# Retention in 128-token chunks with carried states, x^T kept in SBUF, and attention interleaved with the expert matmuls

## The chip, the cores and the metric

The kernel runs on one core of a Trainium2 chip. The metric is the device time of one execution in microseconds (us), taken as the median of several runs. The profile is one execution; its span, from the first to the last instruction, is the scale of all times below that carry a position ("at 62 us"). PE is TensorE's matmul stream and PEld its weight loads, DVE is VectorE, ACT is ScalarE, POOL is GpSimd, and SP is SyncE, which here only issues transfers. A letter q (SPq, POOLq) means the sequencer of that engine.

## The reference, cut to what matters

Retention with a decay per head gives x, and x goes through four experts, weighted by normalised probabilities.

```python
# q, k, v: (8 batches, 8 heads, 576 tokens, 64), float32
scores = (1 / sqrt(64)) * q @ k^T
Dmat   = where(i >= j, gamma[h] ** (i - j), 0)         # causal decay
x      = ((scores * Dmat) @ v) -> (4608 tokens, 512)   # heads side by side
p      = probs / (probs.sum(-1) + 1e-9)                # (4608, 4)
out    = sum over e of p[:, e] * (relu(x @ w1[e]) @ w2[e])   # w1 512x1024, w2 1024x512
```

There is no softmax. The decay factors into a part that belongs to the query and a part that belongs to the key, so retention is linear: the tokens before a chunk act on it only through a 64x64 state per head, the sum of k^T v. The changed kernel rests on this.

## The kernel before

The kernel has two stages with DRAM between them. The first computes the whole lower triangle of scores head by head, with 128x128 blocks, and writes x to DRAM. The second reads x back transposed, 512 tokens at a time, and runs the experts.

```python
x_dram = dram.tile([N_moe, Dm], BF16)
for e in range(E):                       # all eight expert matrices first, on POOL
    nc.gpsimd.dma_start(out=wt1, in_=moe_w1[e]...); nc.gpsimd.dma_start(out=wt2, in_=moe_w2[e]...)
for h in range(H):
    # [cut] load q, k (SP) and v (POOL) of this head for all batches; scale by decay; transpose
    for b in range(B):
        for jb in range(n_sblk):         # 5 key blocks
            while off < Ni:              # all queries after the block
                ps = psum_sc.tile([128, 512], FP32, tag="psc")
                nc.tensor.matmul(ps[:tj, :nn], lhsT=kT[:, j0:j0 + tj], rhs=qT[...])
                rr_copy(s_sbuf[:tj, off:off + nn], ps[:tj, :nn])     # ACT and DVE in turn
            nc.vector.tensor_mul(s_sbuf[:tj, :tj], s_sbuf[:tj, :tj], ltri[:tj, :tj])
        for ib in range(n_sblk):
            for jb in range(ib + 1):
                nc.tensor.matmul(out_p[:ti, :D], lhsT=s_sbufs[jb][...], rhs=vv(jb, 0, tj))
            rr_copy(out_sb[:ti, ib * D:(ib + 1) * D], out_p[:ti, :D])
        nc.sync.dma_start(out=x_dram[...], in_=out_sb[...])
for nt in range(n_ntiles):               # 9 blocks of 512 tokens
    for dc in range(n_dchunk):
        nc.sync.dma_start_transpose(out=t[:, :nn], in_=x_dram[n0:n0 + nn, ...])
    # [cut] experts: 8 groups of 4 matmuls (ph), relu on ACT, 4 groups of 8 matmuls (po),
    #       acc += p * po on DVE (ACT for expert 0), store
```

Of the kernel before, what the change touches and what calls it, by code (L numbers as in the profile page):

```python
# [9 lines left out]
FP32 = mybir.dt.float32  # L11
F32R = mybir.dt.float32r
BF16 = mybir.dt.bfloat16
FP8 = mybir.dt.float8e4
Copy = mybir.ActivationFunctionType.Copy
Relu = mybir.ActivationFunctionType.Relu
Exp = mybir.ActivationFunctionType.Exp


@with_exitstack  # L20
def kernel(
# [10 lines left out]
    nc = tc.nc  # L32

    B, H, S, D = q.shape
    N_moe, E = moe_domain_probs.shape
    E_, Dm, F = moe_w1.shape
    assert E == E_
    assert Dm == H * D
    assert N_moe == B * S

    scale = 1.0 / math.sqrt(D)

    dram = ctx.enter_context(tc.tile_pool(name="dram", bufs=1, space=bass.MemoryType.DRAM))
    x_dram = dram.tile([N_moe, Dm], BF16)

    SBLK = 128
    n_sblk = (S + SBLK - 1) // SBLK
    sblk_sizes = [min(SBLK, S - i * SBLK) for i in range(n_sblk)]
    sblk_starts = [i * SBLK for i in range(n_sblk)]

    DCHUNK = 128
    n_dchunk = Dm // DCHUNK
    FCHUNK = 128
    n_fchunk = F // FCHUNK

    wpool = ctx.enter_context(tc.tile_pool(name="wpool", bufs=1))

    actx = ExitStack()
    const = actx.enter_context(tc.tile_pool(name="const", bufs=1))
    ident = const.tile([128, 128], BF16)  # L60
    make_identity(nc, ident)
    ltri = const.tile([128, 128], BF16)
    nc.gpsimd.memset(ltri, 1.0)
    nc.gpsimd.affine_select(out=ltri, in_=ltri, compare_op=mybir.AluOpType.is_ge, fill=0.0,
                            base=0, channel_multiplier=-1, pattern=[[1, 128]])

    gamma_pool = actx.enter_context(tc.tile_pool(name="gamma", bufs=1))
    qk_pool = actx.enter_context(tc.tile_pool(name="qk", bufs=2))
    psum_tr = actx.enter_context(tc.tile_pool(name="psum_tr", bufs=2, space=bass.MemoryType.PSUM))
    psum_sc = actx.enter_context(tc.tile_pool(name="psum_sc", bufs=3, space=bass.MemoryType.PSUM))  # L70
    psum_out = actx.enter_context(tc.tile_pool(name="psum_out", bufs=3, space=bass.MemoryType.PSUM))
    sbuf_bh = actx.enter_context(tc.tile_pool(name="sbuf_bh", bufs=2))
    sc_pool = actx.enter_context(tc.tile_pool(name="sc_pool", bufs=2))

    iota_tile = gamma_pool.tile([128, 1], FP32, tag="iota")
    nc.gpsimd.iota(iota_tile, pattern=[[0, 1]], base=0, channel_multiplier=1,
                   allow_small_or_imprecise_dtypes=True)
    gq_cache = {}
    gk_cache = {}
    for h in range(H):  # L80
        gamma = 1.0 - 2.0 ** (-5.0 - h)
        lg = math.log(gamma)
        for sb in range(n_sblk):
            s0 = sblk_starts[sb]
            bq = gamma_pool.tile([128, 1], FP32, tag=f"bq_{h}_{sb}")
            nc.vector.memset(bq, lg * s0 + math.log(scale))
            gq = gamma_pool.tile([128, 1], FP32, tag=f"gq_{h}_{sb}")
            nc.scalar.activation(gq, iota_tile, Exp, scale=lg, bias=bq)
            bk = gamma_pool.tile([128, 1], FP32, tag=f"bk_{h}_{sb}")
            nc.vector.memset(bk, -lg * s0)  # L90
            gk = gamma_pool.tile([128, 1], FP32, tag=f"gk_{h}_{sb}")
            nc.scalar.activation(gk, iota_tile, Exp, scale=-lg, bias=bk)
            gq_cache[(h, sb)] = gq
            gk_cache[(h, sb)] = gk

    w1_sb = {}
    w2_sb = {}
    for e in range(E):
        wt1 = wpool.tile([128, n_dchunk, F], BF16, tag=f"w1_{e}", name="wt1")
        nc.gpsimd.dma_start(out=wt1, in_=moe_w1[e].rearrange("(dc p) f -> p dc f", p=128))  # L100
        w1_sb[e] = wt1
        wt2 = wpool.tile([128, n_fchunk, Dm], BF16, tag=f"w2_{e}", name="wt2")
        nc.gpsimd.dma_start(out=wt2, in_=moe_w2[e].rearrange("(fc p) d -> p fc d", p=128))
        w2_sb[e] = wt2

    NB2 = B // 2
    _ci = [0]

    def rr_copy(out_, in_):
        i = _ci[0] % 2  # L110
        _ci[0] += 1
        if i == 0:
            nc.scalar.activation(out_, in_, Copy)  # L113
        else:
            nc.vector.tensor_copy(out_, in_)  # L115

    for h in range(H):
        qT_big = [sbuf_bh.tile([128, S], BF16, tag=f"qT{bb}", name=f"qT{bb}") for bb in range(NB2)]
        kT_big = [sbuf_bh.tile([128, S], BF16, tag=f"kT{bb}", name=f"kT{bb}") for bb in range(NB2)]
        v_raw = {}  # L120
        for sb in range(n_sblk):
            s0 = sblk_starts[sb]
            ts = sblk_sizes[sb]

            def load_scaledT(src, gtile, name, dst):
                raw = qk_pool.tile([128, B, D], FP32, tag=f"{name}_raw{sb}")
                nc.sync.dma_start(out=raw[:ts], in_=src[:, h, s0:s0 + ts, :].rearrange("b s d -> s b d"))
                scaled = qk_pool.tile([128, B * D], BF16, tag=f"{name}_s{sb}")
                nc.scalar.activation(scaled[:ts], raw[:ts].rearrange("p b d -> p (b d)"), Copy,  # L129
                                     scale=gtile[:ts, :])  # L130
                for bb in range(NB2):
                    pt = psum_tr.tile([128, 128], BF16, tag="pt")
                    nc.tensor.transpose(pt[:128, :ts], scaled[:ts, bb * 128:(bb + 1) * 128], ident[:ts, :ts])  # L133
                    rr_copy(dst[bb][:128, s0:s0 + ts], pt[:128, :ts])

            load_scaledT(q, gq_cache[(h, sb)], "q", qT_big)
            load_scaledT(k, gk_cache[(h, sb)], "k", kT_big)

            vr = qk_pool.tile([128, B, D], BF16, tag=f"v_raw{sb}")
            nc.gpsimd.dma_start(out=vr[:ts], in_=v[:, h, s0:s0 + ts, :].rearrange("b s d -> s b d"))  # L140
            v_raw[sb] = vr.rearrange("s b d -> s (b d)")

        for b in range(B):
            bb = b // 2
            ph = (b % 2) * 64
            qT = qT_big[bb][ph:ph + 64, :]
            kT = kT_big[bb][ph:ph + 64, :]

            def vv(sb, r0, rn):
                return v_raw[sb][r0:r0 + rn, b * D:(b + 1) * D]  # L150

            out_sb = sbuf_bh.tile([128, n_sblk * D], BF16, tag="out_sb")
            s_sbufs = []
            for jb in range(n_sblk):
                j0 = sblk_starts[jb]
                tj = sblk_sizes[jb]
                Ni = S - j0
                s_sbuf = sc_pool.tile([128, S], BF16, tag=f"ssb{jb}")
                off = 0
                while off < Ni:  # L160
                    nn = min(512, Ni - off)
                    ps = psum_sc.tile([128, 512], FP32, tag="psc")
                    nc.tensor.matmul(ps[:tj, :nn], lhsT=kT[:, j0:j0 + tj],  # L163
                                     rhs=qT[:, j0 + off:j0 + off + nn], start=True, stop=True)
                    rr_copy(s_sbuf[:tj, off:off + nn], ps[:tj, :nn])
                    off += nn
                nc.vector.tensor_mul(s_sbuf[:tj, :tj], s_sbuf[:tj, :tj], ltri[:tj, :tj])  # L167
                s_sbufs.append(s_sbuf)
            for ib in range(n_sblk):
                i0 = sblk_starts[ib]  # L170
                ti = sblk_sizes[ib]
                out_p = psum_out.tile([128, D], FP32, tag="po")
                for jb in range(ib + 1):
                    j0 = sblk_starts[jb]
                    tj = sblk_sizes[jb]
                    i_off = i0 - j0
                    nc.tensor.matmul(out_p[:ti, :D], lhsT=s_sbufs[jb][:tj, i_off:i_off + ti],  # L177
                                     rhs=vv(jb, 0, tj),
                                     start=(jb == 0), stop=(jb == ib))
                rr_copy(out_sb[:ti, ib * D:(ib + 1) * D], out_p[:ti, :D])  # L180
            n_full = S // SBLK
            rem = S - n_full * SBLK
            nc.sync.dma_start(
                out=x_dram[b * S:b * S + n_full * SBLK, h * D:(h + 1) * D].rearrange("(sb p) d -> p sb d", p=SBLK),
                in_=out_sb[:SBLK, :n_full * D].rearrange("p (sb d) -> p sb d", d=D))
            if rem > 0:
                nc.sync.dma_start(
                    out=x_dram[b * S + n_full * SBLK:b * S + S, h * D:(h + 1) * D],
                    in_=out_sb[:rem, n_full * D:n_full * D + D])

    actx.close()

    NTILE = 512
    n_ntiles = (N_moe + NTILE - 1) // NTILE
# [98 lines left out]
```

## Time and profile before

| what | before |
|---|---|
| time, median (range) | 893.84 us (893.67 to 896.29) |
| span, granted clock | 893.0 us, 1.000 |
| start, PE mostly idle | 0 to 76 us |
| attention | 76 to 384 us |
| round trip of x | 384 to 391 us |
| experts | 391 to 889 us |

The first fence is the windows view of the kernel before. Each line is a stretch of time, its length, then busy time and count of instructions of PE, PEld, DVE, ACT and POOL, then granted clock (the share of TensorE's full clock that it was given), the mean busy share of the DMA engines (which can exceed 1 where transfers overlap), and GB/s.

```profile
0.00:30.00 30.00, 1.97 (x9) 0.97 (x10) 3.23 (x84) 19.24 (x88) 10.51 (x20) 1.00 1.08 185
30.00:60.00 30.00, 3.24 (x13) 1.36 (x13) 1.44 (x7) 5.42 (x14) 4.83 (x6) 1.00 1.27 192
60.00:76.00 16.00, 7.42 (x39) 3.30 (x39) 4.25 (x21) 6.46 (x21) 0.93 (x2) 1.00 1.56 169
76.00:384.00 308.00, 265.30 (x1604) 130.66 (x1603) 170.65 (x803) 171.91 (x553) 25.18 (x30) 1.00 0.52 75
384.00:391.00 7.00, 3.72 (x8) 1.10 (x9) 0.00 (x0) 0.00 (x0) 0.00 (x0) 1.00 0.40 86
391.00:889.00 498.00, 497.75 (x2297) 225.00 (x2295) 96.94 (x215) 196.49 (x324) 0.00 (x0) 1.00 0.09 27
```

Three stages have three limits. Until 76 us the DMA is full and PE waits. From 76 to 384 us PE is busy 86% of the time, with 1604 small matmuls. From 391 us PE is never idle, and DVE and ACT are busy only 19% and 39% of that time, so there is room for other work beside the experts.

The second fence is the chain of waits of the kernel before where the stages meet: start, length, what, and how many instructions.

```profile
388.75 2.63 DMA t<-x_dram
391.42 7.23 PE ph L240 x24
398.65 6.91 PE po L249 x32
```

Thirty-two matmuls of 512 columns take 6.91 us, that is 216 ns each. There are 2304 of them, hence 497 us, which the change does not touch. Everything else in the kernel, 396 us of 893, is what a change can win.

### The profile page before, as it was taken

How to read it: one execution, taken by the hardware profiler on the slowest of the kernel's cores; microseconds unless marked ns; L12 is line 12 of the kernel's file. 1: busy time of each engine (PE TensorE's matmuls, PEld its weight loads, DVE VectorE, ACT ScalarE, POOL GpSimd, SP SyncE). 2: the span in 40 equal slices, each digit the busy share in tenths (PEclk: the TensorE clock that was granted, in tenths of full speed). 3: DMA queues.
4: the chain of work that ended last, by engine and by line, in shares of the span. 5: the costliest groups of instructions: out<-in, count | busy, mean ns of one | idle time of the engine just before them, and what ended most of it. 6: DMA issues, size and time to landing. Idle time of an engine off the chain costs nothing.

```text
span 893.0 us, 11224 instructions
## 1 busy us (share of the span) xinstructions
PE 779.4 (87%) x3968; PEld 362.4 (41%) x3968; DVE 277.3 (31%) x1128; ACT 399.5 (45%) x997; POOL 41.5 (5%) x57
## 2 busy tenths in 40 slices
PE   0016998988788898989999999999999999999998
PEld 0003444444344444434444444444444444444443
DVE  1004555656455554532202212022130211302112
ACT  8125766664646444434352442534425334243342
POOL 4110101011010100000000000000000000000000
PEclk9999999999999999999999999999999999999999
DMA  9999479393945510120110201002020020200101
GB/s 181 199 175 178 75 108 123 73 120 80 114 81 54 44 17 11 21 55 2 36 36 0 72 1 49 23 1 71 1 60 13 1 70 1 71 1 1 47 1 48
DMA packets 187704, 51.67 MB, mean 58 GB/s; under 512 B 176896, under 2 KB 180992, under 8 KB 187648
## 3 DMA queue, kind: packets, MB, share of 16 engines
q1 hardware_dynamic: 143872, 37.84, 20.5%
q0 software_dynamic: 43776, 13.11, 13.5%
q8 instruction: 31, 0.51, 0.2%
q14 instruction: 25, 0.20, 0.1%
HBM read 45.16 MB, written 14.16 MB: 66 GB/s over the span
## 4 chain that ended last, share of the span: by engine, by line
PE 74%; issue 10%; DMA 9%; ACT 4%; DVE 1%; POOL 1%; SPq 1%; POOLq 0%; ACTq 0%
PE ph L240 28%; PE po L249 28%; PE ps L163 9%; PE out_p L177 6%; DMA vr<-in_v_dram 5%; PE pt L133 3%; DMA wt_419<-in_moe_w_dram 2%; ACT s_sbuf L113 2%; DMA raw<-in_k_dram 1%; POOL vr L140 0%; SPq L212 0%; DMA t<-x_dram 0%; DVE s_sbuf L115 0%; DVE s_sbuf L167 0%; DVE out_sb L115 0%
## 5 line engine op out<-in xcount | busy, mean ns | idle before, releaser
L244 ACT ACTIVATE hT<-ph 128x512 bf16<-128x512 f32 x288 | 171.8, 597 | 264.4 <-PE ph L240 264.4
L257 DVE SCALAR_TENSOR_TENSOR acc<-po,p_t,acc 128x512 f32<-128x512 f32 x108 | 81.0, 750 | 378.8 <-PE po L249 378.8
L249 PEld LDWEIGHTS <-hT 128*128 128x128 bf16 x1152 | 112.8, 98 | 135.8
L133 PE MATMUL pt<-ident,scaled 128*128 128x128 bf16 (+1 forms) x320 | 69.5, 269 | 87.9 <-ACT scaled L129 17.9
L177 PE MATMUL out_p<-vr,s_sbuf 128*128 128x64 bf16 (+2 forms) x960 | 113.2, 242 | 6.0 <-ACT out_sb L113 5.0
L177 PEld LDWEIGHTS <-s_sbuf 128*128 128x128 bf16 (+2 forms) x960 | 70.2, 127 | 86.9 <-issue 49.3
L113 ACT ACTIVATE s_sbuf<-ps 128x512 bf16<-128x512 f32 (+2 forms) x192 | 74.7, 391 | 67.5 <-PE ps L163 63.6
L115 DVE CAST s_sbuf<-ps 128x64 bf16<-128x64 f32 (+2 forms) x192 | 80.5, 427 | 13.1 <-PE ps L163 8.7
L133 PEld LDWEIGHTS <-scaled 128*128 128x128 bf16 (+1 forms) x320 | 32.0, 115 | 109.0 <-issue 85.4
L240 PE MATMUL ph<-t,wt_415 128*128 128x512 bf16 x288 | 67.7, 393 | 3.9 <-DMA t<-x_dram 3.9
L240 PE MATMUL ph<-t,wt_427 128*128 128x512 bf16 x288 | 63.6, 379 | 0.0
L249 PE MATMUL po<-wt_417,hT 128*128 128x512 bf16 x288 | 63.6, 379 | 0.0
L249 PE MATMUL po<-wt_421,hT 128*128 128x512 bf16 x288 | 63.6, 379 | 0.0
L240 PE MATMUL ph<-t,wt_419 128*128 128x512 bf16 x288 | 63.6, 379 | 0.0
L249 PE MATMUL po<-wt_425,hT 128*128 128x512 bf16 x288 | 63.6, 379 | 0.0
L240 PE MATMUL ph<-t,wt_423 128*128 128x512 bf16 x288 | 63.6, 379 | 0.0
L249 PE MATMUL po<-wt_429,hT 128*128 128x512 bf16 x288 | 63.6, 379 | 0.0
L167 DVE TENSOR_TENSOR s_sbuf<-s_sbuf,ltri 128x128 bf16<-128x128 bf16 (+1 forms) x320 | 59.3, 208 | 11.8 <-ACT s_sbuf L113 9.9
L115 DVE CAST out_sb<-out_p 128x64 bf16<-128x64 f32 (+1 forms) x160 | 34.1, 218 | 66.1 <-PE out_p L177 60.3
L113 ACT ACTIVATE out_sb<-out_p 128x64 bf16<-128x64 f32 (+1 forms) x160 | 34.3, 222 | 35.3 <-PE out_p L177 26.1
L140 POOL DMA_DIRECT2D vr<-in_v_dram x40 | 33.6, 854 | 265.7 <-PE pt L133 117.0
L240 PEld LDWEIGHTS <-wt_415 128*128 128x128 bf16 x288 | 28.9, 101 | 41.1 <-issue 9.4
(159 smaller groups left out, 471.8 us busy)
## 6 DMA issues: line engine op xcount, KB each, us to landing
out_dram<-acc SPq DMA_DIRECT2D x36, 256.0 KB, 2.1
raw<-in_q_dram SPq DMA_DIRECT2D x32, 256.0 KB, 5.3
raw<-in_k_dram SPq DMA_DIRECT2D x32, 256.0 KB, 5.6
vr<-in_v_dram POOLq DMA_DIRECT2D x32, 128.0 KB, 6.8
x_dram<-out_sb SPq DMA_DIRECT2D x64, 64.0 KB, 1.8
wt_415<-in_moe_w_dram POOLq DMA_DIRECT2D x1, 1024.0 KB, 10.7
wt_417<-in_moe_w_dram POOLq DMA_DIRECT2D x1, 1024.0 KB, 16.5
wt_419<-in_moe_w_dram POOLq DMA_DIRECT2D x1, 1024.0 KB, 21.4
```

Source lines behind the costliest of these rows:

```text
L113: nc.scalar.activation(out_, in_, Copy)
L115: nc.vector.tensor_copy(out_, in_)
L133: nc.tensor.transpose(pt[:128, :ts], scaled[:ts, bb * 128:(bb + 1) * 128], ident[:ts, :ts])
L140: nc.gpsimd.dma_start(out=vr[:ts], in_=v[:, h, s0:s0 + ts, :].rearrange("b s d -> s b d"))
L163: nc.tensor.matmul(ps[:tj, :nn], lhsT=kT[:, j0:j0 + tj], rhs=qT[:, j0 + off:j0 + off + nn], start=True, stop=True)
L167: nc.vector.tensor_mul(s_sbuf[:tj, :tj], s_sbuf[:tj, :tj], ltri[:tj, :tj])
L177: nc.tensor.matmul(out_p[:ti, :D], lhsT=s_sbufs[jb][:tj, i_off:i_off + ti], rhs=vv(jb, 0, tj), start=(jb == 0), stop=(jb == ib))
L240: nc.tensor.matmul(ph[:128, :nn], lhsT=w1e[:, dc, fc * FCHUNK:(fc + 1) * FCHUNK], rhs=xt_tiles[dc][:, :nn], start=(dc == 0), stop=(dc == n ...
L244: nc.scalar.activation(hT[:, fc, :nn], ph[:, :nn], Relu)
L249: nc.tensor.matmul(po[:nsn, :], lhsT=hT[:, fc, ns * NSUB:ns * NSUB + nsn], rhs=w2e[:, fc, :], start=(fc == 0), stop=(fc == n_fchunk - 1))
L257: nc.vector.scalar_tensor_tensor(acc_tiles[ns][:nsn, :], po[:nsn, :], p_tiles[ns][:nsn, e:e + 1], acc_tiles[ns][:nsn, :], op0=mybir.AluOpT ...
```

## The change

The intent is to do less attention work, to drop the DRAM copy of x, and to put attention into the gaps of DVE and ACT beside the experts. Retention is done in chunks of 128 tokens: scores only inside a chunk, and a state carried from chunk to chunk. Two heads share one PE array: score matmuls use one half of its rows each (64x128), output matmuls one half of its columns each (128x64). Outputs come out transposed, so they go straight into x^T. Attention of batch nt+1 is cut into 19 units, one placed after every second expert group of block nt.

```diff
-    x_dram = dram.tile([N_moe, Dm], BF16)
+    xT = const.tile([128, NDC, N], BF16)
...
+        def U_kv(n, pairs):          # state: k^T v of chunk n added up in PSUM, copied by ACT
+            nc.tensor.matmul(kvp[g][:, p, :], lhsT=km[:, n, ...], rhs=vm[:, n, ...], ...)
+            nc.scalar.activation(sbd[n][j:j + 64, a:z, j:j + 64], kvp[g][...], Copy)   # j = 0, 64
+        def U_T(p):                  # 8 transposes of q and k for a pair of heads
+            nc.tensor.transpose(pt[:, i, c * C:(c + 1) * C], src[:, c, ...], ident)
+            nc.vector.tensor_copy(qkT[:, :, p, 0:SM], pt)
+        def U_S(p):                  # scores inside the chunks
+            for c in range(NC_):
+                for j in range(2):   # two heads, two row halves of the array
+                    r = slice(64 * j, 64 * j + 64)
+                    nc.tensor.matmul(s[j][:, c, :], lhsT=qkT[r, 1, p, cs], rhs=qkT[r, 0, p, cs])
+            nc.vector.tensor_tensor(st[:, j], s[j], tri..., op=MULT)
+        def U_O(p):                  # scores x v, plus state x q; decay on the way out
+            nc.tensor.matmul(o[64 * j:64 * j + 64, ...], lhsT=vm[:, c, 2 * p + j, :], rhs=sT[p][:, j, c, :])
+            nc.tensor.matmul(o[:, ...], lhsT=sbd[c - 1][:, p, :], rhs=qkT[:, 0, p, ...])
+            nc.vector.tensor_tensor(xT[:, p, b * S:b * S + SM], o, gq[:, p, 0:SM], op=MULT)
...
-            nc.sync.dma_start_transpose(out=t[:, :nn], in_=x_dram[n0:n0 + nn, ...])
+    att = attention(0)               # batch 0 alone, before the experts
+    for nt in range(n_nt):
+        nxt = attention(nt + 1) if nt + 1 < B else None
+        if nxt is not None and nt + 2 < B:
+            load(nt + 2)
+        for _ in moe(nt):            # yields after each of 48 expert groups
+            n += 1
+            if nxt is not None and n >= 3 and n % 2 == 1:
+                next(nxt, None)
```

The four further matmul groups for the last 64 tokens of a batch (576 = 4 x 128 + 64) are cut here. Loads also change: q, k and v now come batch by batch. Batch 0 comes by SP in 128 KB pieces and is cast by ACT, DVE and POOL; later batches' k comes by SP, their q and v by POOL. The eight expert matrices are still issued by POOL at the very start. PSUM now gives three buffers instead of eight to the experts.

## The prediction

> **What bounds the kernel now.** By the windows view there are three stages. (1) To about 76 us, the DMA: PE is busy 22 of the first 90 us. Eight weight loads (16.8 MB of f32 source) are issued in 9 us and land 5.7 to 6.7 us apart until 57 us; the 256 KB q/k loads, in 256-byte rows, then land every 7 to 9 us, and every 2.7 us afterwards, beside v. (2) 76 to 384 us: attention, PE 86% busy with small matmuls, an eviction and a mask after each. (3) 391 to 889 us: the experts. The chain of waits shows blocks of 32 matmuls at 6.91 us without a gap (216 ns each; 2304 of them, 497 us). The change leaves this work as it is.
>
> **What it removes.** Stage 2 as a stage (308 us) and the round trip of x (385 to 391 us). The chunked form has about 152 small matmuls per batch, against 1664 in all (3968 - 2304 on the page). They run between expert groups, where DVE (18% busy in stage 3) and ACT (40%) have room.
>
> **What it costs on PE.** Five back-to-back 128x64 matmuls take 0.45 us against 0.24 for one (52 ns each); two transposes 0.37 to 0.40 against 0.27 (100 to 130 ns). My estimate is 80 ns: 152 x 0.08 = 12.2 us per batch, plus 1.3 for changes of array shape. The Trainium skill, "TensorEngine Tiling (Array Packing)", Key Properties, says that changing the tiling mode drains the engine; no duration of it can be read here. So 13.5 us per batch; batches 1 to 7 are on the PE path: 94 us.
>
> **The start**, the weak part. Batch 0 needs 3.1 MB on the SP queue in competition with the same weights. The Trainium skill, "DMA: Bandwidth & Descriptors", Issuing engines are not separate DMA queues, says that all queues interleave on the same 16 engines; this trace agrees (7 to 9 us per load beside the weights, 2.7 after). By 58 us some 9 of its 12 x 256 KB are there, the rest by 65 us. In the built order a DVE multiply of batch 1's k stands before batch 0's last x^T write, and PE has batch 1's state matmuls (needing its v) before the first expert group's end. So the experts wait for batch 1's k and v too: the probabilities come as 4608 pieces of 16 bytes ahead of k, and Pool issues v only after its casts. Some 17000 pieces at 195 GB/s of 256 bytes (both queues after 57 us) are 22 us: the experts start in earnest at about 88 us.
>
> **Sum.** 88 start + 494 experts (some are done earlier) + 94 attention + 8 PE bubbles (three PSUM buffers, not eight) + 4 tail = 688 us. Range 655 to 730. Chances: faster by over 2% 0.98, within 2% 0.01, slower 0.01.
>
> **What would show each step.** Windows: PE continuously busy only from 80 to 100 us. Waits: DVE's k multiply of batch 1 waits for its DMA, PE behind it. A block of 512 tokens takes 66 to 73 us, the last one 55 to 56; 512-column matmuls keep 216 ns. DMA nearly idle after 130 us.
>
> **What would make it wrong.** Attention matmuls cheaper by overlapping array tiles (8 us per batch: 650) or dearer by drains (18 us: 720); expert groups waiting for evictions behind attention work on DVE; later q/v loads, issued by Pool one head at a time (0.9 us each), coming too late; a start at 70 or 110 us.

## The result

The changed kernel takes 641.61 us (median of 4 runs, 640.12 to 642.94); the kernel before took 893.75 us (893.47 to 896.29) in the same rounds. The ratio is 0.7175, with a 95% interval from 0.7158 to 0.7192, and the output is correct. Here and below a ratio is the mean time of one kernel's fast runs over that of the kernel before's fast runs of the same rounds, so it is not quite the ratio of the medians. The direction was predicted, but 641.6 lies below the predicted range of 655 to 730 and 46 us below the predicted sum of 688.

The span is 638.6 us. PE's busy line on the page, first before and then after, shows that PE fell by 212 us and now fills 89% of a shorter span.

```profile
PE 779.4 (87%) x3968; PEld 362.4 (41%) x3968; DVE 277.3 (31%) x1128; ACT 399.5 (45%) x997; POOL 41.5 (5%) x57
```

```profile
PE 567.1 (89%) x3454; PEld 270.7 (42%) x3520; DVE 205.3 (32%) x345; ACT 228.2 (36%) x422; POOL 105.3 (16%) x150
```

(66 of 3520 matmul records are missing after; their weight loads are all there.)

The next fence is the windows view after, with the same columns as before.

```profile
50.00:60.00 10.00, 0.00 (x0) 0.00 (x0) 0.29 (x2) 0.63 (x1) 0.61 (x1) 1.00 1.23 211
60.00:70.00 10.00, 6.03 (x40) 3.07 (x41) 4.93 (x13) 4.00 (x17) 9.09 (x13) 1.00 1.54 146
70.00:80.00 10.00, 6.79 (x80) 4.06 (x80) 7.23 (x13) 3.48 (x16) 6.99 (x10) 1.00 1.82 174
80.00:90.00 10.00, 9.77 (x61) 4.95 (x62) 3.02 (x6) 5.59 (x11) 8.25 (x12) 0.83 1.85 176
150.00:250.00 100.00, 99.19 (x643) 47.89 (x654) 38.40 (x60) 40.46 (x74) 19.93 (x27) 1.00 0.43 52
```

PE is busy without a break from 80 us on. Between 150 and 250 us, in the middle of attention and experts together, it is 99% busy; so beside the experts no eviction holds it up.

How long is a block of 512 tokens? The first expert's results leave PSUM through an ACT instruction that writes acc, and its first occurrence marks each block. The timeline of ACT shows it for two early blocks and for the last two.

```profile
153.04 0.69 ACT L352 ACTIVATE acc<-po,probs 128x512 f32<-128x512 f32 x1 [0.94 <-PE po L348]
216.45 0.69 ACT L352 ACTIVATE acc<-po,probs 128x512 f32<-128x512 f32 x1 [0.94 <-PE po L348]
...
532.81 0.69 ACT L352 ACTIVATE acc<-po,probs 128x512 f32<-128x512 f32 x1 [1.13 <-PE po L348]
588.07 0.69 ACT L352 ACTIVATE acc<-po,probs 128x512 f32<-128x512 f32 x1 [1.13 <-PE po L348]
```

A block with attention in it takes 63.41 us (153.04 to 216.45), and one without takes 55.26 (532.81 to 588.07), which is 256 matmuls of 216 ns. So attention costs 8.16 us per batch, bubbles included. With seven such batches, 57.1 us; nine bare blocks, 497.3 us; the last matmul's end at 634.65; this leaves 80.3 us as the effective start, by which I mean everything on PE's path that is neither an expert block nor attention of batches 1 to 7.

Where the 8.16 us go is read from the chain of waits after, inside one block. These lines are samples of all groups; the lines between them are cut.

```profile
227.24 0.45 PE pt L220 x8
227.69 1.73 PE ph L341 x8
229.41 0.16 PE s_1951 L242
229.57 0.05 PE s_1951 L242
229.63 0.05 PE s_1951 L242
229.69 0.05 PE s_1951 L242
232.44 0.34 PE o L267 x8
232.78 0.27 PE o L271 x3
238.69 0.86 PE ph L341 x4
239.55 0.22 PE kvp L207 x4
241.83 1.83 PE ph L341 x8
```

Eight transposes take 0.45 us and four state matmuls 0.22, that is 56 ns each. Eight score matmuls, of which the chain shows one of each pair, take about 0.33. Eight output matmuls take 0.34 and the three state outputs after them 0.27. Eight 512-column matmuls take 1.73 us after transposes but 1.83 after scores (the score group before 241.83 is cut): the way back from the half-array shape costs 0.1 us. The timeline of PE shows the pairs of score matmuls, on the two row halves, starting together, within 10 ns:

```profile
229.41 0.22 PE L242 MATMUL s_1951<-qkT 64*128 64x128 bf16 x1
229.41 0.22 PE L242 MATMUL s_1952<-qkT 64*128 64x128 bf16 x1
229.47 0.22 PE L242 MATMUL s_1951<-qkT 64*128 64x128 bf16 x1
229.47 0.22 PE L242 MATMUL s_1952<-qkT 64*128 64x128 bf16 x1
```

The start is read from the waits of the changed kernel (in total, how often, longest) and from ACT's timeline.

```profile
ACT qm L192 <- DMA raw_q<-in_q_dram: 39.0, 3, 21.1
PE kvp L207 <- ACT sbd_158 L213: 24.1, 1, 24.1
PE kvp L207 <- DMA vm<-in_v_dram: 2.3, 2, 1.3
```

```profile
58.53 0.63 ACT L192 ACTIVATE qm<-raw_q 128x512 bf16<-128x512 f32 x1 [21.12 <-DMA raw_q<-in_q_dram]
62.18 0.63 ACT L192 ACTIVATE qm<-raw_q 128x512 bf16<-128x512 f32 x1 [3.02 <-DMA raw_q<-in_q_dram]
62.71 0.43 ACT L213 ACTIVATE sbd_158<-kvp 64x64 bf16<-64x64 f32 x2
```

In the built order ACT has all four casts of batch 0's q ahead of the first copy of a state (sbd). The last q lands at 62.2 us, so PE stands from 39 to 63 us and then needs about 17 us for batch 0's attention. The last of the three waits is for batch 1's v: until 80.0 us, state matmuls of batch 1 stand on PE between those of batch 0, and PE waits 2.3 us for their v.

### The profile page after: what moved, and what is told of

Its sections match the earlier page's. It is cut to its first block, busy times and chain, and to the rows that moved or that the text cites. A ratio compares the mean times of both kernels' runs of the same rounds, so it can differ in the third digit from the quotient of the medians.

```text
span 638.6 us, 8366 instructions
## 1 busy us (share of the span) xinstructions
PE 567.1 (89%) x3454; PEld 270.7 (42%) x3520; DVE 205.3 (32%) x345; ACT 228.2 (36%) x422; POOL 105.3 (16%) x150
## 4 chain that ended last, share of the span: by engine, by line
PE 86%; SPq 8%; DMA 3%; issue 1%; POOL 1%; DVE 0%; ACT 0%; ACTq 0%; POOLq 0%
PE po L348 39%; PE ph L341 39%; SPq L79 8%; PE pt L220 2%; PE o L267 2%; DMA vm<-in_v_dram 1%; PE o L271 1%; PE kvp L207 1%; DMA qm<-in_q_dram 1%; DMA raw_v<-in_v_dram 1%; POOL qm L101 1%; PE ptr L229 0%; DVE sTr L259 0%; PE orem L280 0%; PE orem L284 0%
## 5 line engine op out<-in xcount | busy, mean ns | idle before, releaser
L354 DVE SCALAR_TENSOR_TENSOR acc<-po,probs,acc 128x512 f32<-128x512 f32 x108 | 81.1, 751 | 197.8 <-PE po L348 177.6
L341 PE MATMUL ph<-xT,wt_166 128*128 128x512 bf16 x277 | 67.7, 385 | 1.3 <-issue 0.6
L341 PE MATMUL ph<-xT,wt_178 128*128 128x512 bf16 x281 | 68.0, 380 | 0.4
L341 PE MATMUL ph<-xT,wt_174 128*128 128x512 bf16 x277 | 67.5, 380 | 0.5
L101 POOL DMA_DIRECT2D qm<-in_q_dram x56 | 41.6, 775 | 158.4 <-PE pt L220 156.2
L341 PE MATMUL ph<-xT,wt_182 128*128 128x512 bf16 x279 | 66.7, 380 | 0.5
L348 PE MATMUL po<-wt_184,hT 128*128 128x512 bf16 x283 | 63.4, 379 | 0.3
L101 POOL DMA_DIRECT2D vm<-in_v_dram x56 | 41.7, 771 | 60.5 <-PE o L271 58.2
L223 DVE COPY qkT<-pt 128x1024 bf16<-128x1024 bf16 x32 | 22.0, 688 | 90.8 <-PE pt L220 90.8
L220 PE MATMUL pt<-ident,qm 128*128 128x128 bf16 x128 | 13.4, 229 | 34.0 <-ACT qm L192 34.0
L341 PEld LDWEIGHTS <-wt_166 128*128 128x128 bf16 x288 | 27.7, 99 | 31.0 <-issue 1.8
L207 PE MATMUL kvp<-vm,km 128*128 128x128 bf16 x128 | 15.5, 225 | 27.4 <-ACT sbd_158 L213 24.1
L341 PEld LDWEIGHTS <-wt_182 128*128 128x128 bf16 x288 | 26.8, 98 | 29.3
L341 PEld LDWEIGHTS <-wt_174 128*128 128x128 bf16 x288 | 26.4, 98 | 28.8
L341 PEld LDWEIGHTS <-wt_178 128*128 128x128 bf16 x288 | 26.4, 98 | 28.5
L352 ACT ACTIVATE acc<-po,probs 128x512 f32<-128x512 f32 x36 | 24.7, 687 | 36.9 <-PE po L348 36.9
L185 DVE TENSOR_TENSOR km<-raw_k,gk 128x512 bf16<-128x512 f32 (+1 forms) x44 | 22.0, 557 | 36.8 <-DMA raw_k<-in_k_dram 19.6
```

What stands on the lines that cost most here:

```text
L101: nc.gpsimd.dma_start(out=m[:, :, h, :], in_=main_in(src, b, h))
L185: nc.vector.tensor_tensor(km[:, c, h0:h1, :], t["k"][:, c, h0:h1, :], gk[:, c, h0:h1].unsqueeze(2).to_broadcast([128, n, D]), op=MULT)
L207: nc.tensor.matmul(kvp[g][:, p, :], lhsT=km[:, n, 2 * p:2 * p + 2, :].rearrange("p h d -> p (h d)"), rhs=vm[:, n, 2 * p:2 * p + 2, :].rear ...
L220: nc.tensor.transpose(pt[:, i, c * C:(c + 1) * C], src[:, c, 2 * p:2 * p + 2, :].rearrange("p h d -> p (h d)"), ident)
L223: nc.vector.tensor_copy(qkT[:, :, p, 0:SM], pt)
L341: nc.tensor.matmul(ph, lhsT=w1_sb[e][:, dc, fc * 128:(fc + 1) * 128], rhs=xT[:, dc, n0:n0 + NT], start=(dc == 0), stop=(dc == NDC - 1))
```

## The experiments

Three questions were open: why attention is so cheap on PE (a1, a2, a3, a5), what sets the start (a4, b1, b2), and whether a better start can be had (c1 to c5). Except for a4, all outputs were correct. Every run had three rounds beside the kernel before.

| run | what it does | median, us (range) | ratio to before (95%) |
|---|---|---|---|
| a1 | transposes of batches 1 to 7 done twice | 653.17 (652.72 to 654.19) | 0.7315 (0.7304 to 0.7325) |
| a2 | scores: one row half, then the other | 640.96 (640.60 to 641.25) | 0.7176 (0.7164 to 0.7188) |
| a3 | each score group in two | 646.16 (645.22 to 649.26) | 0.7240 (0.7221 to 0.7260) |
| a4 | attention of batch 0 alone (wrong) | 581.57 (581.42 to 581.78) | 0.6511 (0.6502 to 0.6521) |
| a5 | the two row halves in separate groups | 653.29 (652.31 to 654.25) | 0.7314 (0.7294 to 0.7333) |
| b1 | PE, ACT, DVE held to the written order | 638.14 (637.78 to 638.36) | 0.7144 (0.7126 to 0.7161) |
| b2 | experts 1 to 3's weights after batch 0's loads | 632.60 (629.39 to 633.96) | 0.7077 (0.7050 to 0.7103) |
| c1 | b1 and b2, and batch 1 later | 611.07 (607.66 to 613.35) | 0.6850 (0.6823 to 0.6876) |
| c2 | c1 with a shorter chain for batch 0 | 608.74 (608.47 to 609.03) | 0.6818 (0.6806 to 0.6829) |
| c3 | c2 with POOL held to the written order | 613.24 (612.13 to 614.10) | 0.6865 (0.6848 to 0.6883) |
| c4 | c3 with batch 1 between the weights | 606.35 (606.04 to 607.55) | 0.6793 (0.6780 to 0.6805) |
| c5 | c4, later, and fewer early loads | 600.99 (599.23 to 601.71) | 0.6720 (0.6706 to 0.6734) |

### a1: what one small matmul costs

```diff
-                for c in range(NC_):
+                for c in [c for c in range(NC_) for _ in range(1 if first else 2)]:   # in U_T
```

> The 32 full transposes of each of batches 1 to 7 are done twice, right result. Theory A (a small matmul with new weights costs PE only what its 128 columns take when nothing makes it wait: eight transposes stand in 0.45 us of the chain, 56 ns each): a block of 512 tokens grows from 63.4 by 32 x 0.056 = 1.8 to 65.2 us, the run by 12.5 us to about 654. Rival B (the prediction's step: 80 to 130 ns each, weight load and columns one after the other): blocks of 66.0 to 67.6 us, the run 18 to 29 us longer.

The block grew from 63.41 to 65.19 us, by 1.78 us for 32 added transposes: 56 ns each. The chain of waits of a1 shows sixteen where eight were:

```profile
231.44 0.89 PE pt L220 x16
```

So a back-to-back 128-column matmul with its own weight load costs 56 ns, not the 80 ns of my estimate. The Trainium skill, "TensorE: Matmul & The Clock Gate", Part 1, gives a gap of about 56 ns for back-to-back 128x128x128 matmuls at full clock; the run agrees. I should have looked there when the trace before offered two readings, 52 ns and 100 to 130 ns, and I took a value between them.

### a2, a5: the two halves of the array

```diff
# a2, in U_S
-            for c in range(NC_):
-                for j in range(2):
+            for j in range(2):
+                for c in range(NC_):
# a5: U_S(p) becomes two units, U_S(p, (0,)) and U_S(p, (1,)), each with an expert group after it
-            for c in range(NC_):
-                for j in range(2):
+            for c in range(NC_):
+                for j in js:
```

> Within a score unit the four matmuls of the upper 64 rows come first, then the four of the lower 64 rows, instead of in turns; same work, right result. Theory A (two neighbours on different halves of the array rows run at once, which is why the chain shows 0.00 us for every second one): the unit loses the overlap, about 0.055 x 4 = 0.22 us each, 0.9 us per block (64.3 us), the run 6 us longer. Rival B (the second of a pair is cheap for another reason, such as the order of the records): no change, 63.4 us.

> The score run with the order of the halves changed showed no loss: its trace still has the matmuls starting two at a time, so the engine takes them out of the written order. Here the two halves of a score unit stand in different units with expert matmuls between, so that they can't meet. Four more units per batch, as in the run with split score units (646.2 us, pairs kept). Theory A (two halves of the rows at once are what makes a score matmul cost 28 ns): 4 x 4 x 0.055 = 0.9 us per block more than that run, 6 us in all, about 652. Rival B (a 64-row matmul of 128 columns takes 28 ns by itself): as that run, 646.

In a2 the block took 63.45 us, that is nothing changed, and the expected loss of 6 us did not come. The built instruction stream does have four matmuls of one half, then four of the other. Yet the trace has eight score matmuls in the time of four. The first fence is the timeline of PE in a2, the second in a5, where only one half is at hand:

```profile
229.55 0.41 PE L242 MATMUL s<-qkT 64*128 64x128 bf16 x8
```

```profile
225.43 0.39 PE L246 MATMUL s<-qkT 64*128 64x128 bf16 x4
```

Eight took 0.41 us in a2 and four took 0.39 us in a5. The single records of a2 start in pairs: 229.552 and 229.565, 229.618 and 229.632, 229.674 and 229.688, 229.730 and 229.743. The record does not name the half, but its semaphores tell it. In the built program the first matmul of each half carries a wait, and the fourth of each half an update; these are the first, fifth, fourth and eighth as written. In the trace, in all 28 score groups of batches 1 to 7, the first two to start carry the waits and the last two the updates. So PE started matmuls of the second half ahead of earlier-written ones of the first. (In a5, where all four are on one half, the starts are some 55 ns apart.) The premise of a2 (written order is start order) fell.

a5 gave the answer that a2 could not, since an expert group stands between the halves. Its block took 65.13 us, 0.88 us over a3, which has the same number of changes of array shape. These are 16 matmul slots of 55 ns that had been shared by two halves. So a pair on two row halves costs one slot, 28 ns each, and this was shown by taking the pairing away.

### a3: what a change of array shape costs

```diff
-                      lambda: U_S(0), lambda: U_kv(2, allp), lambda: U_T(2), lambda: U_S(1),
+                      lambda: U_S(0, (0, 1)), lambda: U_S(0, (2, 3)), lambda: U_kv(2, allp), ...
```

(The same for the other pairs; each half is its own unit, with expert matmuls after it.)

> Each score unit is cut in two, with expert matmuls between the halves: the same matmuls, but four more entries into and exits from the 64-row array shape per batch. Theory A (a change of shape costs about 0.1 us on the way in and 0.1 on the way out, as the chain's 0.16 for a first score matmul and 1.83 instead of 1.73 after it suggest): 0.8 us more per block (64.2 us), the run 5.6 us longer. Rival B (changes of shape are free; those 0.1 us are the pipeline's filling that is overlapped): 63.4 us.

The block took 64.25 us, 0.84 more, for four added entries into the half-row shape and four exits from it: 0.21 us for each in and out. The chain of waits of a3 shows both parts:

```profile
230.88 0.22 PE s L246 x4
231.10 0.97 PE ph L347 x4
```

Two pairs, 0.11 us of work, took 0.22; four 512-column matmuls took 0.97 us where they take 0.86 otherwise (238.69 in the chain after, above). The Trainium skill, "TensorEngine Tiling (Array Packing)", Key Properties, says that a change of tiling mode drains TensorE. The runs agree that it costs something and give the size that the page lacks.

With these the 8.16 us add up, if each group off the whole array costs what a3's did: there are eleven per batch (five of scores, five of outputs, and the transposes of the last 64 tokens, on 64 rows), 11 x 0.21 = 2.3 us, and the 152 matmuls share the remaining 5.85 us, 38 ns each on average. That fits 60 matmuls of 128 columns on the whole array at 56 ns (3.4 us), 64 that go in pairs at 28 ns (1.8 us), and 28 of the last 64 tokens, with 64 columns, whose single or paired starts are 29 to 32 ns apart in the trace (0.6 us): 5.8 us. For the output matmuls, which pair on column halves, this is read from the chain (eight in 0.34 us, as for scores) and was not tried by itself; nor was the price of a change of shape for any group but the scores.

### a4: is batch 1 on the path of the start?

```diff
-                                     rhs=xT[:, dc, n0:n0 + NT], start=(dc == 0), stop=(dc == NDC - 1))
+                                     rhs=xT[:, dc, 0:NT], start=(dc == 0), stop=(dc == NDC - 1))
-    load(1)
-        nxt = attention(nt + 1) if nt + 1 < B else None
+        nxt = None
```

> Only batch 0 is loaded and attended; all expert blocks read its x^T (wrong result on purpose). Theory A (the attention of batches 1 to 7 is 7 x 8.15 us on PE, and the wait for batch 1's q and v in the start about 5 us): all blocks 55.3 us, experts under way from about 75 us, the run 578 us. Rival B (the start is limited by the weights and batch 0 alone less, so that it falls more, to 65 us): 569 us. Rival C (the attention fits into gaps that PE has anyway, so that its PE time isn't what it costs): over 600 us.

Every block reads batch 0's x^T, so the result is wrong. All blocks took 55.25 us, the last matmul ended at 575.85, and the effective start is 575.85 - 497.3 = 78.5 us. In the changed kernel it was 80.3. So batch 1's data, which I had made responsible for the start, costs at most 2 us; batch 0's own loads and attention make the rest. Even these 2 us may be in part the clock: from 80 to 90 us it was granted at 0.83 in the changed kernel and at 1.00 in a4.

### b1, b2: two ways to an earlier start

b1 keeps PE, ACT and DVE in the order in which the program is written, so that state copies are not behind all casts. b2 leaves the order and delays weights.

```diff
# b1: every PE, ACT and DVE instruction of attention and experts is held to the written order;
#     the normalisation of the probabilities moves behind batch 0's attention
+                keep(nc.tensor.matmul(...))
# b2
-    for e in range(E):
-        load_w(e)
-        if e == 0:
-            load_first_rem()
+    load_w(0)
+    load_first_rem()
...
+    for e in range(1, E):
+        load_w(e)
     load(1)
```

> PE, DVE and ACT keep the order in which the program is written (in the changed kernel ACT has all four q casts of batch 0, and DVE all its k multiplies, before the first eviction of batch 0's states; the transfers are unchanged). Theory A (batch 0's attention stood behind its last load because of that order: PE idle from 39 to 63 us, then 17 us of attention): batch 0 is done about 6 us after its last load at 62, experts from about 69; batch 1's v at 79 costs some 4 us of that; 634 us. Rival B (the prediction's step: batch 1's k and v are what the experts wait for, so that order within batch 0 is worth nothing): 640 us.

> The weights of experts 1 to 3 are issued behind batch 0's v casts, so that batch 0 competes with those of expert 0 only. Theory (batch 0 is slow because the weights share its 16 engines): its last q lands at about 30 us instead of 62, the experts begin at about 45; but batch 1's q and v now come behind six weight transfers, at about 84 us, and PE waits for them in the middle of the first block: in all only some 8 us won, 634 us. Rival (256-byte rows are slow by themselves, 7 to 9 us per 256 KB): last q after 50 us, no gain or a loss.

b1 gained only 3.5 us. Pairs 2 and 3 of heads still get their q at about 60 us, and then the written order takes 5.7 us per pair, one after the other (ACT's casts of q at 60.16 and 65.86). Neither theory had that second part.

In b2 batch 0's last v landed at 29.8 us and its last q at 39.0 instead of 62.1, as ACT's timeline of b2 shows:

```profile
39.11 0.63 ACT L190 ACTIVATE qm<-raw_q 128x512 bf16<-128x512 f32 x1 [4.04 <-DMA raw_q<-in_q_dram]
```

The theory had said about 30: the build put expert 1's first matrix on the queue at 27.1 us, just ahead of the last pieces of q. So it was the competition with the weights that held batch 0. The Trainium skill, "DMA: Bandwidth & Descriptors", Issuing engines are not separate DMA queues, says that transfers of all issuers interleave on the same 16 engines; this run agrees, with 23 us as the price here. But the time fell by 9 us, not by 23. The waits of b2 up to 90 us tell why:

```profile
DVE psm L160 <- DMA probs<-in_moe_domain_probs_dram: 28.7, 1, 28.7
PE s L240 <- DVE qkT L221: 25.3, 2, 22.8
```

DVE had the normalisation of the probabilities ahead of a copy that PE needs, and the probabilities, 4608 pieces of 16 bytes, landed 37 us after issue beside the weights (5.7 us in the changed kernel, where they come after the weights). The total was expected; the wait that made it was another one, so the hit was luck.

### c1, c2: both together, and a shorter chain

c1 joins b1's order with b2's delay, issues transfers in the order of need (expert 0's weights, batch 0, expert 1's, batch 1's q and v, experts 2 and 3's) and starts batch 1's attention only at step 18 of the first block. c2 also overlaps the pairs of heads of batch 0, finishes batch 0's last 64 tokens inside the first block, starts batch 1's attention at step 22, and means to put expert 0's second matrix behind batch 0's casts.

```diff
# c1
+    load_w(0)
+    load_first_rem()
...
+    load_w(1)
     load(1)
+    load_w(2)
+    load_w(3)
-            if nxt is not None and n >= 3 and n % 2 == 1:
+            if nxt is not None and (n >= 18 and n % 3 != 2 if nt == 0 else n >= 3 and n % 2 == 1):
# c2, batch 0
+            for p in range(NP):
+                cast_first(p)
+                if p > 0: U_kv(2, [p - 1])
+                U_T(p)
+                if p > 0: U_kv(3, [p - 1]); U_O(p - 1)
+                U_kv(0, [p]); U_S(p); U_kv(1, [p])
```

> Both together, and transfers in the order of need: expert 0, batch 0, expert 1, batch 1's q and v, experts 2 and 3; batch 1's attention goes into the second half of the first block. If both theories of the start hold: experts from about 37 us and no long wait behind it, 598 us. If batch 1's data or the later weights still come too late: 610 to 625.

> As the run with both changes of the start (611 us, experts from 45 us, with 5.7 us per pair of heads of batch 0 on a chain of matmul, eviction, matmul although its loads had landed by 29 us), with three changes: batch 0's steps of neighbouring pairs in turns, its last 64 tokens (which the first expert block doesn't read) moved behind the first expert groups, and the second weights of expert 0 issued after half of batch 0's casts. Theory A (this chain is what is left of the start): experts from about 32 to 36 us, 597 to 601 us. Rival B (batch 1's or the later weights' transfers are close behind and take it back): PE waits inside the first block, 605 us or more.

c1 came to 611.1 us, inside its rival's range. Batch 0's last v was there at 28.9 us and its last q at 32.6, but ACT's timeline of c1 shows a cast of q every 5.7 us (at 22.95, then as below), for one pair of heads after the other:

```profile
28.65 0.63 ACT L187 ACTIVATE qm<-raw_q 128x512 bf16<-128x512 f32 x1
34.34 0.63 ACT L187 ACTIVATE qm<-raw_q 128x512 bf16<-128x512 f32 x1
```

These two wait for no load: batch 0's own chain of small steps is the limit there. c2 shortens that chain, yet took 608.7 us, which is not clear of c1 (their intervals overlap). POOL's timeline of c2 shows what happened:

```profile
18.17 0.89 POOL L159 DMA_DIRECT2D wt<-in_moe_w_dram  x1
20.82 0.62 POOL L195 CAST vm<-raw_v 128x512 bf16<-128x512 f32 x1 [1.76 <-DMA raw_v<-in_v_dram]
21.38 0.77 POOL L113 DMA_DIRECT2D wt<-in_moe_w_dram  x1
37.07 0.62 POOL L195 CAST vm<-raw_v 128x512 bf16<-128x512 f32 x1 [14.93 <-DMA raw_v<-in_v_dram]
```

POOL's instructions were not held to an order, so the build put two weight matrices ahead of the last cast of v, and the last v landed at 37 us behind them. The competition of b2 had come back by another way.

### c3, c4, c5: the order of POOL's transfers

c3 holds POOL to an order: batch 0 first, then all weights, then batch 1's q and v. c4 puts batch 1's q and v between expert 1's and 2's weights. c5 puts them between expert 2's and 3's, and leaves later batches one buffer for k instead of three, so that k for batches 2 to 4 is not fetched early.

The diffs are condensed.

```diff
# c3 against c2 (all POOL transfers and casts also held to this order)
-    load_w(1); load(1); load_w(2); load_w(3)
+    load_w(1); load_w(2); load_w(3); load(1)
-    n >= 22 and n % 4 != 2 if nt == 0
+    n >= 37 if nt == 0
# c4 against c3
-    load_w(1); load_w(2); load_w(3); load(1)
+    load_w(1); load(1); load_w(2); load_w(3)
-    n >= 37 if nt == 0
+    n >= 22 and n % 4 != 2 if nt == 0
# c5 against c4
-    load_w(1); load(1); load_w(2); load_w(3)
+    load_w(1); load_w(2); load(1); load_w(3)
-    n >= 22 and n % 4 != 2 if nt == 0
+    n >= 33 if nt == 0
-        t["k"] = raw.tile([128, NC_, H, D], FP32, tag="raw", name="raw_k")       # three buffers
+        t["k"] = raw.tile([128, NC_, H, D], FP32, tag="raw_k", name="raw_k")     # one buffer
```

> c2 with GpSimd's transfers held to a written order (expert 0's first matrix, batch 0's four v casts, then the other weights, then batch 1's q and v), and batch 1's attention at every step from n = 37 of the first block. Theory A (what held c2 at 608.7 was pair 3's v arriving at 37 us behind two weight matrices): all of batch 0 lands by 24 to 27 us, experts start at 31 to 36 us, some 4 us of batch 1's attention stays unhidden, 595 to 600 us. Rival B (the first 85 us are bound by the sum of the transfers, so an earlier start is given back as waits for weights or for batch 1's data in the first block): experts start by 36 us all the same, but the first block lengthens by as much, 605 us or more.

> c3 with batch 1's q and v loads moved from behind the last weights to between expert 1's and expert 2's weights, and batch 1's attention from step 22 of the first block on. In c3 the experts started early (first eviction of a finished group at 45 us against 56 in c2) but PE then stood from about 80 to 92 us for batch 1's q, which GpSimd could issue only one piece per landed weight matrix, and the first block took 81.5 us. Theory A (that order of issue alone made the loss): experts start as in c3, the first block takes 64 to 70 us, 594 to 602 us. Rival B (the sum of bytes before about 85 us is the limit, whatever the order): PE waits for expert 2's or 3's weights instead, the first block takes 75 us or more, 605 us or more.

> c4 with batch 1's q and v placed between expert 2's and expert 3's weights, its attention from step 33 of the first block, and one buffer instead of three for later batches' k, so that the k of batches 2 to 4 (some 3.7 MB that nobody needs yet, moved before 110 us in c4) stay out of the DMA's way. In c4 PE stood from about 63 to 73 us for expert 2's first matrix, which GpSimd could issue only at 60 us, behind 16 small loads, since no more than 8 of its transfers are under way at once. Theory A (the order of issue and unneeded transfers lose the time): first block 64 to 69 us, 594 to 602 us. Rival B (the needed bytes alone bound it): first block 72 us or more, 603 us or more.

| run | first acc eviction, us | first block, us | time, us |
|---|---|---|---|
| c2 | 55.75 | 65.45 | 608.74 |
| c3 | 45.12 | 81.54 | 613.24 |
| c4 | 44.70 | 75.38 | 606.35 |
| c5 | 44.24 | 70.03 | 600.99 |

(From the second block on, all four have blocks of 63.40 to 63.41 us.) All of c3 to c5 start the experts 11 us earlier, as theory A said, and pay it back in the first block, as theory B said. For c3, POOL's timeline shows how:

```profile
30.14 0.95 POOL L117 DMA_DIRECT2D wt<-in_moe_w_dram  x1
31.02 0.83 POOL L102 DMA_DIRECT2D qm<-in_q_dram  x1
36.88 0.74 POOL L102 DMA_DIRECT2D qm<-in_q_dram  x1 [5.04 <-DMA wt<-in_moe_w_dram]
```

POOL issues seven weight matrices (from 25.28 to 30.14) and one piece of q, then nothing until the first matrix has landed, then one piece for each landed transfer. In c4 it stops after three matrices and five pieces, in c5 after five and three. That is eight transfers each time, whatever their size. This is the program's own doing: the build gives POOL's transfers eight semaphores in turn, and in the trace each transfer from the ninth on waits for the semaphore of the one eight before it. So what is queued behind the weights cannot even be issued: batch 1's last v was issued at 84 us, and PE, busy 10.00 us in each window of 10 us from 40 to 70, was busy 2.06 us from 80 to 90. In c4 the small pieces are ahead, and expert 2's first matrix, issued at 60 us, came too late; the waits of c4 up to 130 us say so:

```profile
PE ph L335 <- DMA wt<-in_moe_w_dram: 7.5, 1, 7.5
```

c5 is a compromise between the two, and PE is busy for 96% of its span, more than in any other run. Its first block still takes 6.6 us more than the others. PE waits 1.5 us for a weight matrix, and about 3.8 us (99.5 to 103.2 in the chain of waits) pass at the block's end with the rest of batch 1's attention, which has no expert groups left beside it. The clock adds to it: in c3 to c5 it was granted at 0.5 during and after such waits of PE (84.5 to 98.1 and 115.2 to 118.6 us in c3, 67.3 to 77.5 in c4, 103.7 to 107.1 in c5), and 512-column matmuls then started 427 ns apart instead of 216. So these waits cost more than their own length: some 1.5 us more in c5 (7 such matmuls), 3.4 in c3 (16). c5's time lies in theory A's range, its first block between the two theories (70.0 against at most 69 or at least 72). c5 changed two things at once, so how much of its 5 us over c4 came from the order and how much from k is open.

By the two ratios, each to the kernel before, c5 takes 0.672 / 0.7175 = 0.937 of the changed kernel's time, and beats both kernels.

## Why the prediction was wrong, point by point

The prediction was a sum: 88 start + 494 experts + 94 attention + 8 bubbles + 4 tail = 688. The same terms by the trace are 80.3 + 497.3 + 57.1 (attention with its bubbles) + 4.0 = 638.7, the span (80.3 is what the others leave, so the sum closes by itself). The profiled execution took 640.5, 1.9 us above its span; the median is another 1.1 above that.

| term | predicted, us | measured, us |
|---|---|---|
| start, less 3 us of experts done early | 85 | 80.3 |
| experts | 497 | 497.3 |
| attention of 7 batches | 94 | 57.1 with bubbles |
| PE bubbles | 8 | in the line above |
| tail | 4 | 4.0 |

- **The step that failed is "My estimate is 80 ns: 152 x 0.08 = 12.2 us per batch".** The matmuls cost some 38 ns on average, 5.85 us per batch. Two causes were shown: a whole-array matmul of 128 columns costs 56 ns (a1), and two on different row halves cost as much as one (a5). A third, that 28 of the 152 have only 64 columns, is read from the trace alone. I had the first two in hand: 52 ns in the trace before, and "overlapping array tiles (8 us per batch: 650)" in the list of what would make it wrong. That figure for the batch, 8 us, is what was measured; I had given it too little weight.
- **"plus 1.3 for changes of array shape" was too low**, but small: eleven groups at 0.21 us (a3) are 2.3 us.
- **"8 PE bubbles (three PSUM buffers, not eight)" did not occur.** PE is 99% busy in mid-kernel, and 8.16 us per batch are explained by matmuls and changes of shape.
- **"the experts start in earnest at about 88 us" was 5 us too late, for a partly wrong reason.** The last q landed at 62 us (predicted: by 65). But then batch 0's own attention takes 17 us, and batch 1's data counts 2 us at most (a4). The sign I named, DVE's multiply of batch 1's k waiting with PE behind it, is not in the trace; PE's wait for batch 1's v, which I had also named, is, but at 2.3 us. So that the start came near the predicted one is in part luck.
- **What held:** the stages before; the 216 ns and the last block (predicted 55 to 56 us, measured 55.26); PE busy without a break from 80 us (predicted 80 to 100). The block of 63.4 us fell out of the predicted 66 to 73.
- **"DMA nearly idle after 130 us" was wrong**, without effect on the time: the mean share of the DMA engines is 0.43 from 150 to 250 us, since batches stream in until late.

What the experiments do not settle: why PE starts matmuls of the other row half ahead of earlier ones, and how c5's two edits share its gain.

## What to carry to other kernels

Cost small matmuls by the slots they fill: count whole-array matmuls at the back-to-back rate, pairs on different halves once (shown here for row halves), and add the changes of array shape; two times from a trace that differ by a factor of two are two situations, not a range to take the middle of. In the start of a kernel, ask in what order bytes are needed and hold the queues to it, since a large transfer issued early can delay the small ones behind it (b2, c2). When an earlier start gives nothing, look in the next block for the wait that took it back.

## What the Trainium skill lacked or had wrong

- "TensorE: Matmul & The Clock Gate", Back-to-back issue gap, states sustained 81 ns for 128 columns and 131 ns for 512 in streams of weight load and matmul. Here, with a weight load for every matmul, 128 columns took 56 ns (a1) and 512 columns 216 ns (all experts): the page's figures for the isolated gap (56 and 216 ns) are the ones that hold.
- "TensorE: Matmul & The Clock Gate", Part 3, The mechanism, says that matmuls start strictly in order, with no reordering. In a2, four on one row half written before four on the other started with them in pairs, 13 ns apart, and the eight took 0.41 us where four alone take 0.39 us (a5).
- "TensorEngine Tiling (Array Packing)", Key Properties, says that a change of mode drains TensorE but gives no time: 0.21 us for one entry and exit between streams of 512-column matmuls (a3).
- "DMA: Bandwidth & Descriptors" says that queues share the engines but gives no time for a queue of small rows beside one of large transfers: batch 0's last q landed at 62 us beside eight weight matrices and at 39 us when six of them were issued from 27 us on (b2); 4608 pieces of 16 bytes took 37 us beside the weights and 5.7 us after them.
